# Two-layer decode block: the pass between layers in halves, another route for its q, and new order tables

## The chip, the core and the metric

The kernel runs on one core of one Trainium2 chip. The metric is the device time of one execution in microseconds, lower is better. A core has five engines with a queue each, worked off strictly in order: PE (TensorE, matrix products into the accumulation banks, PSUM), DVE (VectorE), ACT (ScalarE), POOL (GpSimd) and SP (SyncE, which here only issues DMA transfers from HBM to the on-chip memory, SBUF). Engines wait for each other through semaphores.

## The reference

Four sequences, one token each, pass through two layers; both layers use the same weights and the same caches.

```
for layer in (0, 1):
    q = layernorm(x) @ wq                       # 512 -> 32 heads x 128
    s = q . k_cache / sqrt(128)                 # 8 kv heads, 4 q heads on each, 4096 keys
    x = x + (softmax(s) . v_cache) @ wo         # 4096 -> 512
    n = layernorm(x)
    x = x + (sigmoid(n @ w_gate) * (n @ w_up)) @ w_down   # 512 -> 1792 -> 512
```

All arrays are bfloat16. K and V of one sequence and one kv head are 1 MiB each; there are 4 x 8 of each.

## The kernel before

**Tiles and slots.** K and V come in whole 1 MiB loads into 12 slots of SBUF, and later also into the four quarters of the tile that holds wq, once wq is needed no more (`yield_wq`). A table (`KEPT`) says which K and V of layer 0 stay in their slots until layer 1 uses them; the rest are loaded twice. wo (8 loads), w_gate, w_up and w_down stay resident. In all SP issues 115 loads, and two of the four short stores at the end.

**Order.** Nothing is ordered at run time. Three tables of letters fix everything. `ORDER` lists the 32 pairs of units as layer, sequence, pair (a unit is one kv head of one sequence). `LOADS` is the order of the transfers. `PROGRAM` is the order in which steps are issued, one letter each: `s` and `z` scores of the first and second unit of a pair, `t`, `u`, `T` parts of the transposition of a K on DVE, `m` `p` `n` `e` the maximum, its spreading, the bias and the exponentials, `P` `C` `D` the transposition of the probabilities and its copies, `h` `r` `i` the sums, `a` half a unit of probabilities times V, `o` (at the end `N`) the normalisation, `w` products with wo, `f` `F` `l` the turning of their result, `b` the block layout of q for a pair, and `.` the next step of a pass. After every letter `pump` issues each load of `LOADS` whose slot has been given up; SP then waits until the last reader of the slot has finished.

**The pass.** When a sequence has finished layer 0, a pass of 18 steps (`pass_steps`) brings it to layer 1: layer norm (`ln_a`, `ln_b`), gate product (`gate_row`), up product (`up_row`), `h_turn`, w_down (`down`, two parts), layer norm again, then q for layer 1. Products with one row as the stationary operand (128 x 1) are put on four strips of 32 columns of the array: each strip holds its own part of the outputs, in output rows 0, 32, 64 and 96 of a bank. `strips` is the constant with the four columns of the identity that pick these rows. There are four passes, spread over layer 0 and the first part of layer 1.

- `up_row` (L857-882): 16 matmuls a pass; then one DVE operation on 128 x 512 forms (tanh + 1) x up in `row_sb[:, 0]` (L877).
- `h_turn` (L884-903): four matmuls turn these rows to columns in one bank, one DVE copy (L899).
- `down` (L990-1018): 56 matmuls of one column; the first part makes output chunks 0 and 1, the second 2 and 3; one DVE operation adds the result to x.
- `first_q` (L929-933): q of the first pair of units needed in layer 1, 16 matmuls of 256 columns on four strips (L908) and a DVE copy. `first_turn` (L935-941): two matmuls (L922) and a DVE copy (L938) make columns of it. `first_spread` (L1022) with `spread_of` (L959): eight matmuls (L963) bring these to the layout that `b` reads.
- `other_half` (L943): the other kv half, 16 matmuls of 512 columns, ACT copy. `other_quarter` (L947): the remaining quarter, 16 matmuls of 256 columns on four strips (L908), DVE copy of 128 x 256 (L950). `others_turn` (L953): six matmuls and a copy. `others_spread` (L1034): 16 matmuls and an ACT copy. The last pass's `other_quarter` is the last reader of wq.

**The end.** The last pair's products with V finish layer 1. The last V comes in two halves. Then wo, the last layer norm and the last MLP for all four sequences follow (`last_unit`, `gate`, `up_half`); the change leaves these functions alone.

Of the kernel before, what the change touches and what calls it, by code (L numbers as in the profile page):

```python
# [133 lines left out]
sttzuumtpwnePtub szhubmpDrneTCihP saTazbaa swwmpDneotztCmtrihatPaapanorTCbDia  # L134
saettaawhozrwbixxwPCDmT swfzpaamFlnaeaow.w.pn.hr.P.e..ih.D.CP.aa.aw.a.b. sDrCzTobi.m.u
spzanaePbamphuaCr.on.DiaaaatehPTu soDCzmuxwtbpr sziwnmeaaaapxonbPher shzCwDfTPirwmaapbT
saaFlConzwm.iwtwue..wbDphuaaPraa.tt.w.C sz.n.Dmoe.piahwTabanPw.raCwoi st.zaDam.e.b.h
szptmaPaDoCrnib..w.aapeawaPThruDC.n sozewiabma sphunPaaztCbworewimDpTwaftwahaaFt
sPCroilzbDneahwmapaParoiCnDwaae.aawPhCD.T.Tor. s..zi.mauawpw.neu.bta.awPot.D sCw.hzw.mbw.r
sipzbanetama.apTPthr.CoD stwniezhmaa.P.abpan sCDzorimaTaapbattewP sDzhCnoebrhimtaaPapatDornwC  # L140
seiafaaaPTzohCrFlimapbnDeaaaohwrPCwT.wt swiwt...zD.m.apaanao.e.bhT.rPT sD.iz.C.aawm.pbn.
szmae..aP.h.orbpCw szwDbniehaTaaa smTPzCorTpiDnamaapenPbhraeo stizwDCmpbttnahPDtaaw
sazrCeoiPhaDmrapanaCewowfwwiPFCaaDaahlaoarXaiaNwY
"""


def bass_interleave_layers__gqa_block_cached__glu_gated_glu__decode_kernel(
# [228 lines left out]
    def dve(fn, reads=(), writes=()):  # L376
        return S.inst("dve", fn, reads=reads, writes=writes)
# [479 lines left out]
    def up_row(part):  # L857
        fns = []
        wv = wu_sb.rearrange("p k (f d) -> p k f d", d=2 * P)
        for k in range(2 * part, 2 * part + 2):  # L860
            for st in range(4):
                nt = (KW - st + 3) // 4
                fns.append(
                    (lambda k, st, nt: lambda e: e.matmul(
                        M_ps[1][32 * st:32 * st + 1, 0:nt * 2 * P],
                        lhsT=xc_bf[:, k, 0:1],
                        rhs=wv[:, k, bass.ds(st, nt, step=4), :],
                        start=(k == 0),
                        stop=(k == KD - 1),
                    ))(k, st, nt)  # L870
                )
# [4 lines left out]
        dve(  # L876
            lambda e: e.scalar_tensor_tensor(  # L877
                out=row_sb[:, 0, :], in0=t_row[:, :], scalar=1.0, in1=M_ps[1][:, :], op0=ALU.add, op1=ALU.mult
            ),
            reads=["rc", "rd", "rb", "M1"],  # L880
            writes=["ra"],
        )

    def h_turn():  # L884
        fns = []
        for t in range(2):
            for e_ in range(2):
                fns.append(
                    (lambda t, e_: lambda e: e.matmul(
                        M_ps[0][:, bass.ds(8 * t + e_, 4, step=2)],  # L890
                        lhsT=row_sb[:, 0, bass.ds(2 * P * t + e_, P, step=2)],
                        rhs=strips,
                        start=True,
                        stop=True,
                    ))(t, e_)
                )
        S.group("pe", fns, reads=["ra"] + IDENT, writes=["M0"])
        dve(
            lambda e: e.tensor_copy(hT_bf[:, :, 0], M_ps[0][:, 0:KF]),  # L899
            reads=["M0"],  # L900
            writes=["rc", "rd"],
        )

# [30 lines left out]

    def first_turn():  # L935
        S.group("pe", turned(2 * P, 0, 2), reads=["ra"] + IDENT, writes=["M0"])
        dve(
            lambda e: e.tensor_copy(qT_sb[:, 0:2 * REP], M_ps[0][:, 2 * P:2 * P + 2 * REP]),  # L938
            reads=["M0"],
            writes=["rb"],  # L940
        )
# [5 lines left out]
    def other_quarter(n0):  # L947
        S.group("pe", q_group(M_ps[1], n0 // 2, 2 - 2 * (n0 % 2), 2, range(KD)), reads=Q_READS, writes=["M1"])
        dve(
            lambda e: e.tensor_copy(row_sb[:, 1, 0:2 * P], M_ps[1][:, 0:2 * P]), reads=["M1"], writes=["rc", "rd"]  # L950
        )

    def others_turn():  # L953
        S.group("pe", turned(0, 0, 4) + turned(4 * REP, 1, 2), reads=["ra", "rc", "rd"] + IDENT, writes=["M0"])
# [4 lines left out]
    def spread_of(N, quadrants):  # L959
        S.group(  # L960
# [8 lines left out]
                ))(t, a, 64 * (t // 2) + t % 2)  # L969
                for t in range(NT4) for a in quadrants  # L970
            ],
# [17 lines left out]

    def down(b0, nb, part):  # L990
        xkeys = [f"x{b}" for b in range(b0, b0 + nb)]
        fns = []
        for c in range(2 * part, 2 * part + 2):
            for k in range(KF):
                fns.append(
                    (lambda c, k: lambda e: e.matmul(
                        M_ps[0][:, 128 + c * nb:128 + (c + 1) * nb],
                        lhsT=wd_sb[:, k, cols(c)],
                        rhs=hT_bf[:, k, 0:nb],
                        start=(k == 0),  # L1000
                        stop=(k == KF - 1),
                    ))(c, k)
                )
        rd = ["rc", "rd"] + wkeys["wd"]
        if part == 0:
            S.group("pe", fns, reads=rd, writes=["M0"])
            return
        S.last_write["M0"] = S.group("pe", fns, reads=rd)
        assert nb == 1
        dve(  # L1010
# [3 lines left out]
            ),  # L1014
            reads=["M0", "rs"] + xkeys,
            writes=xkeys,
        )

    def pass_steps(b0):
        n0 = seq[2 * firsts[1, b0]][2] // 2  # L1020

        def first_spread():  # L1022
            spread_of(2 * REP, range(2))
            begun.add(b0)
# [9 lines left out]
        def others_spread():  # L1034
            spread_of(6 * REP, range(4))
            act(
# [15 lines left out]
            h_turn,  # L1052
            lambda: down(b0, 1, 0),
            lambda: down(b0, 1, 1),
            lambda: ln_a(b0, 1),
            lambda: first_q(n0),
            first_turn,
            first_spread,
            second_sums,
# [699 lines left out]
```

## Time and profile before

| | us |
|---|---|
| median of three runs | 304.23 |
| the three runs | 305.87, 304.23, 302.63 |
| the profiled execution | 303.62 |
| its span, first to last instruction | 301.8 |
| PE busy | 218.2 |
| DVE busy | 192.8 |
| ACT busy | 122.0 |
| mean granted TensorE clock | 0.703 of full speed |

The profile is one execution, recorded by the hardware. "Busy" counts the time in which an engine works on an instruction. A row of a group gives source line, engine, operation, output and inputs, shape and count, then the time busy and the mean duration of one in ns, then the idle time just before and what ended it. PE's matmuls are pipelined, so durations of neighbours overlap. The 40 slices are 7.5 us each; a digit is the busy share in tenths, PEclk the granted clock in tenths. In rows of windows the DMA share may exceed 1, since packets overlap.

### The profile page before, as it was taken

To read this page: it belongs to the slowest core of one execution; us is meant where nothing else is said; L and a number is where in the kernel's file an instruction comes from. 1 tells how busy PE (TensorE), PEld (TensorE's weight loads), DVE (VectorE), ACT (ScalarE), POOL (GpSimd) and SP (SyncE) were. 2 spreads that over 40 slices of the span, in tenths; PEclk is the share of its full clock that TensorE was granted. 3 is DMA by queue.
4 is the path that set the end of the run, shared out by engine and by line. 5 is a ranking of instruction groups with operands and counts; after the bars stand their busy time and mean duration, and the time that the engine had idled before them with its cause. 6 is when DMAs were issued, how large, how long until landed. Compare 5 with 4: busy or idle time off the path is not lost. (4 is left out here: it accounts for less than half of the span.)

```text
span 301.8 us, 11397 instructions
## 1 busy us (share of the span) xinstructions
PE 218.2 (72%) x4904; PEld 150.9 (50%) x4904; DVE 192.8 (64%) x447; ACT 122.0 (40%) x421; POOL 42.6 (14%) x213
## 2 busy tenths in 40 slices
PE   1232373136779878797997979988988787888996
PEld 1221242122537555464655566744656564456685
DVE  6376757035543868668765767887585776497553
ACT  1010422410542374434444575325456352456830
POOL 0001111001000202111012110110311010122000
PEclk9999999999995757757565556675555595555555
DMA  7999999999999999999999999999999999999920
GB/s 287 422 427 419 414 395 397 398 384 422 413 404 418 417 421 419 418 410 395 414 372 421 397 418 423 417 417 417 385 421 420 419 393 376 416 418 418 414 95 3
DMA packets 20361, 117.38 MB, mean 389 GB/s; under 512 B 1876, under 2 KB 5976, under 8 KB 7640
## 3 DMA queue, kind: packets, MB, share of 16 engines
q1 hardware_dynamic: 20288, 116.66, 95.3%
q8 instruction: 38, 0.62, 0.8%
q14 instruction: 11, 0.09, 0.1%
q10 hardware_dynamic: 24, 0.01, 0.0%
HBM read 116.66 MB, written 0.00 MB: 387 GB/s over the span
## 5 line engine op out<-in xcount | busy, mean ns | idle before, releaser
L1081 DVE STREAM_TRANSPOSE slot<-slot 128x2048 f32<-128x2048 f32 (+2 forms) x69 | 102.8, 1495 | 29.0 <-DMA slot<-in_A_k_cache_dram 27.4
L1228 ACT ACTIVATE pT<-PT 32x128 bf16<-32x128 f32 x232 | 62.2, 268 | 60.4 <-PE PT L1173 26.5
L1273 PE MATMUL O_ps<-pT,slot 128*128 128x4 bf16 x1856 | 59.1, 166 | 21.3 <-DVE small L1253 12.8
L1273 PEld LDWEIGHTS O_ps<-pT,slot 128*128 128x128 bf16 x1856 | 55.2, 103 | 31.2 <-issue 17.9
L1097 PE MATMUL S_ps<-slot,qz 128*16 128x256 bf16 x992 | 61.4, 395 | 12.9 <-DVE slot L1081 5.8
L1155 ACT ACTIVATE wide<-S_ps,small 128x256 bf16<-128x256 f32 x64 | 33.2, 519 | 38.8 <-DVE small L1146 24.2
L1097 PEld LDWEIGHTS S_ps<-slot,qz 128*16 128x16 bf16 x992 | 27.7, 114 | 31.3 <-DVE slot L1081 9.6
L734 POOL COPY qz<-qs 32x32 bf16<-32x32 bf16 x112 | 22.9, 204 | 124.0 <-PE S_ps L1097 86.7
L1190 POOL TENSOR_TENSOR small<-small 128x8 bf16<-128x8 f32 (+1 forms) x96 | 19.3, 201 | 120.7 <-ACT wide L1155 84.0
L1114 DVE TENSOR_REDUCE small<-S_ps 128x2 bf16<-128x512 f32 x32 | 21.5, 671 | 7.7 <-PE S_ps L1097 5.4
L1173 PE MATMUL PT<-ident_bf,wide 128*128 128x64 bf16 (+1 forms) x288 | 18.4, 224 | 7.9 <-ACT pT L1228 3.8
L1173 PEld LDWEIGHTS PT<-ident_bf,wide 128*128 128x128 bf16 x288 | 14.7, 119 | 13.6 <-ACT wide L1155 5.0
L1139 DVE SCALAR_TENSOR_TENSOR O_ps<-O_ps,small,wide 128x128 f32<-128x128 f32 x32 | 10.9, 342 | 10.3 <-PE O_ps L1123 9.9
L908 PE MATMUL M_ps<-wq,small 128*1 128x256 bf16 (+1 forms) x192 | 15.4, 483 | 1.4 <-issue 1.4
L1330 PE MATMUL AC<-wo,oT 128*1 128x512 bf16 x96 | 11.9, 577 | 5.0 <-DMA wo<-in_A_wo_dram 2.6
L1155 ACT ACTIVATION_READ_ACCUMULATOR wide<-S_ps,small 128x1 f32 x64 | 12.3, 192 | 0.0
L1123 PE MATMUL O_ps<-ident_bf,small 128*128 128x64 bf16 x64 | 8.5, 223 | 5.2 <-DVE small L1114 5.2
L1146 DVE TENSOR_REDUCE small<-O_ps 128x2 f32<-128x128 f32 x32 | 9.3, 292 | 3.1 <-DVE O_ps L1139 0.5
L1123 PEld LDWEIGHTS O_ps<-ident_bf,small 128*128 128x128 bf16 x64 | 4.3, 107 | 11.9 <-DVE small L1114 8.8
L1304 DVE TENSOR_TENSOR oT<-O_ps,small 128x8 bf16<-128x8 f32 (+1 forms) x32 | 5.2, 162 | 6.6 <-PE O_ps L1273 6.4
L908 PEld LDWEIGHTS M_ps<-wq,small 128*1 128x1 bf16 x192 | 5.4, 114 | 7.5 <-issue 5.7
L839 PE MATMUL M_ps<-wg,small 128*1 128x512 bf16 (+1 forms) x64 | 8.2, 558 | 0.9 <-DVE small L503 0.9
(150 smaller groups left out, 198.2 us busy)
## 6 DMA issues: line engine op xcount, KB each, us to landing
slot<-in_A_v_cache_dram SPq DMA_DIRECT2D x50, 1024.0 KB, 9.2
slot<-in_A_k_cache_dram SPq DMA_DIRECT2D x43, 1024.0 KB, 10.3
wq<-in_A_wq_dram SPq DMA_DIRECT2D x2, 2048.0 KB, 9.8
wo<-in_A_wo_dram SPq DMA_DIRECT2D x8, 512.0 KB, 15.9
wq<-in_A_v_cache_dram SPq DMA_DIRECT2D x2, 1024.0 KB, 12.5
wq<-in_A_k_cache_dram SPq DMA_DIRECT2D x2, 1024.0 KB, 12.6
wg<-in_B_w_gate_dram SPq DMA_DIRECT2D x2, 896.0 KB, 12.9
wu<-in_B_w_up_dram SPq DMA_DIRECT2D x2, 896.0 KB, 11.3
```

The lines of the kernel that those rows point to most:

```text
L734: (lambda a, ps: lambda e: e.tensor_copy(qz_sb[ps, :, :, a, :], qs_sb[b][ps, :, c0:c0 + 2 * REP].rearrange("p t (u r) -> p u t r", r=REP), ...
L908: (lambda k, st: lambda e: e.matmul(M[32 * st:32 * st + 1, 0:nj * P], lhsT=xc_bf[:, k, 0:1], rhs=q_rows[:, k, h, j0:j0 + nj, st, :], start ...
L1081: dve(lambda e: e.transpose(kf, kf), writes=[f"s{st}"])
L1097: (lambda t, b2, e_, c, x1, r0: lambda e: e.matmul(S_ps[p][r0:r0 + 4 * REP, half], lhsT=qz_sb[:, part, t, :, :].rearrange("p a r -> p (a r)"),
L1114: dve(lambda e: e.tensor_reduce(rm_bf, S_ps[p].rearrange("p (u n) -> p u n", u=2), AX.X, ALU.max), reads=[f"S{p}"], writes=["rmb"])
L1123: (lambda u: lambda e: e.matmul(O_ps[n][:, P + 64 * u:P + 64 * u + 64], lhsT=rm_bf[:, u:u + 1].broadcast_to([P, P]), rhs=valid_bf, start=T ...
L1155: (lambda u, half: lambda e: e.activation(pe_sb[:, half], S_ps[p][:, half], ACTF.Exp, bias=nm_sb[:, u:u + 1], scale=scale, accum_out=sm_sb ...
L1173: (lambda w, a0, a1, c0: lambda e: e.matmul(PT[:, c0:c0 + 16 * (a1 - a0)], lhsT=wide_sb[:, NV + 64 * w:NV + 64 * w + P], rhs=valid_bf[:, : ...
L1190: (lambda out, a, b, op: lambda e: e.tensor_tensor(out, a, b, op))(out, a, b, op),
L1228: (lambda dst, frm: lambda e: e.activation(dst, frm, ACTF.Copy))(dst, frm),
L1273: (lambda n, x, c, j: lambda e: e.matmul(bank[:, ul * REP:(ul + 1) * REP], lhsT=vv[:, x * JG + c * 4 + j, :], rhs=pT[:, x % 2, ul, j, 2 * ...
L1330: (lambda r, h, i: lambda e: e.matmul(AC[32 * r:32 * r + 1, :], lhsT=oT_sb[:, h, own_column:own_column + 1], rhs=wo_sb[:, h, :], start=(j ...
```

## The change

1. **Up product in halves.** Two DVE operations of 128 x 256 take the place of one of 128 x 512; the second writes to the other half of `row_sb`.
2. **`h_turn` in halves.** Its four matmuls become two groups of two, one into each of the banks M0 and M1, and there are two copies, of 8 and of 6 columns, into `h_pass`.
3. **`down` in halves of the contraction.** Part 0 takes the first 8 of 14 chunks of h for all four output chunks, part 1 the other 6. It is still 56 matmuls.
4. **First pair's q.** `first_turn` and its copy go. `first_spread` takes the rows themselves as the stationary operand: 16 matmuls of four columns. A pass has 17 steps now.
5. **Last quarter of q.** 8 matmuls of 512 columns on two strips; the DVE copy takes 128 x 512; its turn takes four matmuls where it took two.
6. **New tables** `ORDER`, `LOADS` and `PROGRAM`. `KEPT` stays, and with it the set of loads. Among the pairs, 100 and 102 change places, 121 goes ahead of 111, and 133 ahead of 131. wo and the MLP weights come earlier in `LOADS`; at its end the last three K are loaded next to each other, before the last seven V.

```diff
 ORDER = """
-003 002 001 000 011 013 101 010 012 102 100 022 021 023 112 020 110 103 030 032 120 031 123 033 111
-121 113 131 133 130 132 122
+003 002 001 000 011 013 101 010 012 100 102 022 021 023 112 020 110 103 030 032 120 031 123 033 121
+111 113 133 131 130 132 122
 """
 LOADS = """
-kkkvkkvkkk oovkovvovk oogookkvvu guddvvkkvv kkvvkkvvvk vkvkvkvvkv vkvvkkvvvk kkvvkvvkkv vkkvkvkvvv
-kkvvkkvkvv kvkvkkvvvv vv
+ovkkokovko kkvvokkkkk oovvovkuvg guddvvkkvv kkvkvkvvkv vkvkvkvvvv kkvvkkvvvk kvkvkkvvvk vkkvkvvkvv
+kkvkvkvkvv kvkkkvvvvv vv
 """
 PROGRAM = """
...
-szmae..aP.h.orbpCw szwDbniehaTaaa smTPzCorTpiDnamaapenPbhraeo stizwDCmpbttnahPDtaaw
-sazrCeoiPhaDmrapanaCewowfwwiPFCaaDaahlaoarXaiaNwY
+s.CD.zmbi..aa.wTp..aan.ehT sPo.z.mb.rpi sCDne..auaha.z.rumPaCoiwpbDn sztmweaapThPaaoDnCbew
+swzrmihbaapaPraCTownwi sezTDmbaahpPnwDaarCoi saePDTzahmapnaCeowriwafFaPalhraCoDaiXaaNwawwY
 """
...
+    h_pass = t_bf[:, 2 * P:2 * P + KF]
...
-        dve(
-            lambda e: e.scalar_tensor_tensor(
-                out=row_sb[:, 0, :], in0=t_row[:, :], scalar=1.0, in1=M_ps[1][:, :], op0=ALU.add, op1=ALU.mult
-            ),
-            reads=["rc", "rd", "rb", "M1"],
-            writes=["ra"],
-        )
+        for n in range(2):
+            cs = slice(2 * P * n, 2 * P * n + 2 * P)
+            part_keys = (["ra"], ["rc", "rd", "rb"])[n]
+            dve(
+                (lambda n, cs: lambda e: e.scalar_tensor_tensor(
+                    out=row_sb[:, n, 0:2 * P], in0=t_row[:, cs], scalar=1.0, in1=M_ps[1][:, cs],
+                    op0=ALU.add, op1=ALU.mult,
+                ))(n, cs),
+                reads=["M1"],
+                writes=part_keys,
+            )
 
     def h_turn():
...
+        for t in range(2):
+            ks = slice(8 * t, min(8 * t + 8, KF))
+            dve(
+                (lambda t, ks: lambda e: e.tensor_copy(h_pass[:, ks], M_ps[t][:, ks]))(t, ks),
+                reads=[f"M{t}"],
+                writes=[f"h{t}"],
+            )
...
-    def first_turn():
-        S.group("pe", turned(2 * P, 0, 2), reads=["ra"] + IDENT, writes=["M0"])
-        dve(
-            lambda e: e.tensor_copy(qT_sb[:, 0:2 * REP], M_ps[0][:, 2 * P:2 * P + 2 * REP]),
-            reads=["M0"],
-            writes=["rb"],
+    def first_spread():
+        S.group(
+            "pe",
+            [
+                (lambda t, j, a: lambda e: e.matmul(
+                    M_ps[1][32 * a:32 * a + 32, 8 * t + 4 * j:8 * t + 4 * j + 4],
+                    lhsT=row_sb[:, 0, bass.ds(P * j + 64 * (t // 2) + t % 2, 32, step=2)],
+                    rhs=strips,
+                    start=True,
+                    stop=True,
+                ))(t, j, a)
+                for t in range(NT4) for j in range(2) for a in range(2)
+            ],
+            reads=["ra"] + IDENT,
+            writes=["M1"],
         )
...
     def other_quarter(n0):
-        S.group("pe", q_group(M_ps[1], n0 // 2, 2 - 2 * (n0 % 2), 2, range(KD)), reads=Q_READS, writes=["M1"])
-        dve(
-            lambda e: e.tensor_copy(row_sb[:, 1, 0:2 * P], M_ps[1][:, 0:2 * P]), reads=["M1"], writes=["rc", "rd"]
-        )
+        h, j0 = n0 // 2, 2 - 2 * (n0 % 2)
+        S.group(
+            "pe",
+            [
+                (lambda k, st: lambda e: e.matmul(
+                    M_ps[1][32 * st:32 * st + 1, :],
+                    lhsT=xc_bf[:, k, 0:1],
+                    rhs=q_rows[:, k, h, j0:j0 + 2, 2 * st:2 * st + 2, :],
+                    start=(k == 0),
+                    stop=(k == KD - 1),
+                ))(k, st)
+                for k in range(KD) for st in range(2)
+            ],
+            reads=Q_READS,
+            writes=["M1"],
+        )
+        dve(lambda e: e.tensor_copy(row_sb[:, 1, :], M_ps[1][:, :]), reads=["M1"], writes=["rc", "rd", "rb"])
...
-    def down(b0, nb, part):
+    def down(b0, part):
+        fns = [
+            (lambda c, k: lambda e: e.matmul(
+                M_ps[0][:, 128 + c:129 + c],
+                lhsT=wd_sb[:, k, cols(c)],
+                rhs=h_pass[:, k:k + 1],
+                start=(c == 0 and k == 0),
+                stop=(c == KD - 1 and k == KF - 1),
+            ))(c, k)
+            for c in range(KD) for k in range(8 * part, min(8 * part + 8, KF))
+        ]
```

More of the change, by code (lines that the diff above doesn't have):

```diff
@@ L969, in spread_of @@
                 ))(t, a, 64 * (t // 2) + t % 2)
[L970 removed]
+                for t in range(NT4) for a in range(4)
             ],
@@ L988, in scales @@
         )
-    def down(b0, nb, part):
[L991 to L1004, printed above, removed]
+    def down(b0, part):
[8 more added lines that the diff above has]
+            for c in range(KD) for k in range(8 * part, min(8 * part + 8, KF))
+        ]
         if part == 0:
-            S.group("pe", fns, reads=rd, writes=["M0"])
+            S.group("pe", fns, reads=["h0"] + wkeys["wd"], writes=["M0"])
             return
-        S.last_write["M0"] = S.group("pe", fns, reads=rd)
-        assert nb == 1
+        S.last_write["M0"] = S.group("pe", fns, reads=["h1"] + wkeys["wd"])
         dve(
```

64 lines of the change are left out of this document (34 added, 30 removed).

## The prediction

> **What bounds the kernel now.** I began with the page: busy shares, the 40 slices, the queues.
>
> ```profile
> span 301.8 us, 11397 instructions
> PE 218.2 (72%) x4904; PEld 150.9 (50%) x4904; DVE 192.8 (64%) x447; ACT 122.0 (40%) x421; POOL 42.6 (14%) x213
> ...
> PE   1232373136779878797997979988988787888996
> ...
> PEclk9999999999995757757565556675555595555555
> DMA  7999999999999999999999999999999999999920
> GB/s 287 422 427 419 414 395 397 398 384 422 413 404 418 417 421 419 418 410 395 414 372 421 397 418 423 417 417 417 385 421 420 419 393 376 416 418 418 414 95 3
> ...
> q1 hardware_dynamic: 20288, 116.66, 95.3%
> ```
>
> The DMA row stands at 9 from the second slice to the 38th, so the kernel is a stream of 116.66 MB with a tail behind it. Undisturbed slices move some 422 GB/s: a 1 MiB load, which is one K or V, takes 1.049 MB / 422 = 2.48 us of stream. PE is close behind from slice 13 on, at a granted clock of 0.5 to 0.7. Next, the windows: the steady stretch first whole, then cut where slices of the GB/s row dip.
>
> ```profile
> 93.00:260.00 167.00, 141.39 (x3121) 96.63 (x3121) 118.64 (x276) 79.60 (x276) 27.42 (x135) 0.59 1.01 409
> ...
> 140.00:172.00 32.00, 28.35 (x643) 19.46 (x644) 22.21 (x54) 16.13 (x57) 6.29 (x31) 0.60 1.00 399
> 203.00:217.00 14.00, 11.79 (x262) 7.55 (x254) 8.37 (x16) 7.58 (x26) 2.62 (x13) 0.50 1.00 402
> 239.00:259.00 20.00, 16.48 (x351) 10.88 (x347) 14.77 (x41) 6.91 (x23) 2.02 (x10) 0.67 0.99 389
> ```
>
> The columns are length, busy time of PE, weight loads, DVE, ACT and POOL, then clock, DMA share and GB/s. Against 422 GB/s, 167 us at 409 lose 5.1 us. Three stretches hold most of it: 32 x (1 - 399/422) = 1.7 us, 14 x (1 - 402/422) = 0.7 us, 20 x (1 - 389/422) = 1.6 us. Over the whole stretch PE idles 167 - 141.4 = 25.6 us, and DVE 48.4 us. Last, what makes a dip: the SP queue's timeline, one landing, and the chain of waits.
>
> ```profile
> 239.47 3.19 SPq L373 DMA_DIRECT2D slot<-in_A_k_cache_dram  x2
> ...
> slot<-in_A_k_cache_dram SPq DMA_DIRECT2D x1, 1024.0 KB, 6.3
> ...
> 242.33 6.80 DMA slot<-in_A_k_cache_dram
> 249.13 0.02 issue
> 249.15 2.31 DVE slot L1081
> ```
>
> The first K, issued at 239.47, took 6.3 us and landed at 245.8. The next was issued at 242.33, only 3.4 us before that, and landed at 249.13: 3.4 us behind its predecessor instead of 2.48. So a slot that comes free late costs up to a microsecond, though a load is still in flight. The chain then stays on compute to the end: stream and PE are both near their limit.
>
> **A rule weighed.** The Trainium skill, "DMA: Bandwidth & Descriptors" (the two cost components), puts the fixed cost of a transfer at some 2.0 us, so that an issue 3.4 us ahead should leave no gap. The measured gap differs, and the measurement decides. By the page the tables could gain or lose nothing through issue times; that is part of the third rival.
>
> **The change, part by part.** The sum starts at the profiled execution's 303.62 us (its span is 301.8), 0.6 below the median of 304.23 and inside the runs' 302.63 to 305.87.
>
> *The last quarter of q.* Each of four passes turns 16 matmuls of 256 columns on four strips into 8 of 512 on two; its copy grows from 256 to 512 columns.
>
> ```profile
> 252.34 1.06 PE L908 MATMUL M_ps<-wq,small 128*1 128x256 bf16 x16
> ...
> 258.15 2.73 PE L908 MATMUL M_ps<-wq,small 128*1 128x512 bf16 x32
> ...
> L908 PE MATMUL M_ps<-wq,small 128*1 128x256 bf16 x128 | 8.5, 412 | 1.4 <-issue 1.4
> L877 DVE SCALAR_TENSOR_TENSOR t_row<-t_row,M_ps 128x512 bf16<-128x512 f32 x4 | 2.7, 673 | 1.8 <-PE M_ps L864 1.7 <-ACT t_row L852 0.2
> L950 DVE CAST t_row<-M_ps 128x256 bf16<-128x256 f32 x4 | 1.7, 425 | 5.5 <-PE M_ps L908 5.5
> ```
>
> Sixteen matmuls of 412 ns finish in 1.06 us, so four strips run side by side. The group of 32 is 16 of 512 columns and the old quarter's 16: 2.73 - 1.06 = 1.67 us for four rounds of 512 columns. No row has two strips; if two run side by side as four do, the new quarter is again four rounds of 512: 1.67 us, for which 0.85 was spent (half the columns). That is +0.85 us of PE per pass at this clock. The bounds are half of it, at the full clock, and 1.7 us more, if strips do not pair up; I take +0.85, since the 0.5 clock rules where three of four passes stand. DVE gains 0.673 - 0.425 = 0.25, taking L877 as the nearest 512-wide row. Here the Trainium skill speaks the other way: "TensorEngine Tiling (Array Packing)", Instruction Overhead, gives each matmul some 60 cycles of overhead, and by it half as many matmuls would be the cheaper group. The rows show no such overhead between strips, only columns.
>
> In all 4 x 1.1 = 4.4 us on two engines. What hides it is the 25.6 us of PE idle above. That cover is gone in the last pass: there the chain runs through these very matmuls.
>
> ```profile
> 251.52 1.03 PE S_ps L1097 x13
> 252.55 0.89 PE M_ps L908 x15
> 253.43 0.02 issue
> 253.45 0.44 DVE t_row L932
> 253.89 0.05 issue
> 253.94 0.22 PE M_ps L922 x2
> ...
> 258.22 2.66 PE M_ps L908 x32
> ```
>
> I take one pass of four: **+1.1** (0 to +4.4). Queued behind the longer group on PE are score and P·V products, and on SP the four loads that wait for the last quarter to give up wq.
>
> *The first pair's q.* The turn (0.22, L922) and its copy (167 ns below) go, with about 0.1 of hand-over: 0.5 saved. Sixteen spread matmuls stand for eight.
>
> ```profile
> L963 PE MATMUL M_ps<-t_row,ident_bf 128*32 128x8 bf16 x32 | 1.1, 171 | 0.3 <-DVE t_row L938 0.3
> L938 DVE CAST t_row<-M_ps 128x8 bf16<-128x8 f32 x4 | 0.7, 167 | 1.9 <-PE M_ps L922 1.9
> L899 DVE CAST t_row<-M_ps 128x14 bf16<-128x14 f32 x4 | 0.8, 191 | 1.5 <-PE M_ps L889 1.5
> ```
>
> Four passes' eights are busy 1.1 us together, 0.27 each; eight more add at most that, and I take 0.1, since most of 0.27 is one pipe's drain. The gain reaches the path only where nothing else fills PE; in the last pass: **-0.4** (0 to -1.6).
>
> *Halves.* Before, product 0.67, turn some 0.25 (a group as short as L922's 0.22), copy 0.19: w_down can start 1.11 us after the up product. After, two products of 256 columns, each between L950's 0.43 and half of L877's 0.67, and two copies of about 0.17 stand on DVE in the order product, product, copy, copy: the first copy ends at 0.43 + 0.43 + 0.17 = 1.03. The second (1.28) hides under the first half of w_down. Gain 0.08 per pass, against 0.34 more DVE time: **0** (-0.3 to +1.4, if DVE were the bound).
>
> *The tables.* The same 117 issues of SP, the same bytes, the same K and V kept. I counted in both orders of instructions, for each load that reuses a slot, how many loads lie between it and the newest one that its slot's release must wait for. A small number means a late issue. For the 65 loads from the 40th on the mean is 3.88 in both. Two stand in before: loads 61 and 67, inside 140 to 172; after, 61, 67 and also 99, inside the 239 to 259 stretch. Loads 85 and 86 (203 to 217) go from three and three to four and three. By the stretches: +0.9 for a third two (1.7 / 2), -0.7 for the 203 to 217 dip: **+0.2** (-4.0, all three dips closed, to +2.6, three more twos).
>
> *The tail.*
>
> ```profile
> 268.13 0.70 SPq L373 DMA_DIRECT2D slot<-in_A_v_cache_dram  x1
> ...
> slot<-in_A_v_cache_dram SPq DMA_DIRECT2D x1, 512.0 KB, 22.1
> ...
> 290.65 1.07 PE L1273 MATMUL S_ps<-slot,slot 128*128 128x4 bf16 x32
> 291.58 0.57 PE L1423 MATMUL O_ps<-oT,wo 128*128 128x4 bf16 x16
> ```
>
> The last half V lands at 268.13 + 22.1 = 290.2. PE takes it up at 290.65, with both halves' products (0.93) and then w_o of the unit before (0.49) still to do. In the new order half the products and this w_o stand ahead of the last half. Were PE free at the landing, 0.4 + 0.47 + 0.49 = 1.3 us would go. It is late now, but wq's slots are given up two loads earlier and three K loads then go ahead of the last seven V's, so I take **-0.9** (0 to -1.3).
>
> Sum: 303.62 + 1.1 - 0.4 + 0 + 0.2 - 0.9 = 303.6 us.
>
> **Rivals.** *PE sets the pace.* From 93 us on its longer quarter is not absorbed in any pass: +4.4, with +0.9 for load 99 and no gain in the tail: 303.62 + 5.3 = 308.9. For it: PE busy 85% there, and the chain's compute end. Against it: the DMA share of 1.01 in the same row. It decides once the idle that a pass finds is under 1.1 us.
>
> *The tables close the dips.* -4.0, tail -1.3, first pair -0.4: 297.9. For it: the dips are late issues, and several first pair's chains get shorter. Against it: the same mean distance, and one two more.
>
> *Nothing reaches the end.* Dips that are not due to issue times, a tail still limited by PE, every edit under PE idle: 303.6 within 0.5. It lies within the forecast's own range.
>
> **How the numbers follow.** Forecast with the third rival 0.50, own range 301.2 to 306.5; dips closed 0.27; PE's pace 0.23. About 1% is what a measurement tells from no change here. Nearly all of the first case is within that; the second is faster and the third slower. The range, 299.0 to 308.0, leaves a tenth on each side.
>
> **What would show it.** Quarter: eight matmuls in about 1.7 us at the 0.5 clock; under 1.0 refutes me. First pair: its spread directly behind L932's copy. Halves: the first copy behind the second product on DVE. Tables: a gap of about 0.9 us before the 99th load's landing; GB/s in the three stretches near 399, 402, 389. Tail: w_o of the last pair's first unit ahead of the last half V. I am wrong if those stretches rise above 415, or if PE's idle from 93 to 260 falls by 4 us and the stream's GB/s with it.

## The result and the profile after

The changed kernel takes 306.73 us (median of 20 runs, 303.81 to 310.53); the kernel before, on the same chip, takes 303.98 (20 runs, 302.63 to 307.26). The ratio is 1.0067 with a 95% interval of [1.0043, 1.0092]; it leaves out executions over 1.5% slower than the fastest of their kernel, which is why it lies under the quotient of the medians. The forecast was 303.6 us, a hair from no change. The time is inside its range and inside the 1% that it called no change, but the interval excludes 1: the change costs some 2.0 us.

The profiled execution took 303.81 us, the fastest of the twenty, so its page shows the changed kernel at its best. First the page: span, engines, clock, GB/s by slice, and the queue that carries instructions.

```profile
span 302.0 us, 11426 instructions
PE 221.4 (73%) x4904; PEld 150.3 (50%) x4904; DVE 194.5 (64%) x448; ACT 121.6 (40%) x421; POOL 42.4 (14%) x213
...
PEclk9999999999995766557567556855665575757555
...
GB/s 296 405 409 404 411 403 420 391 410 417 413 400 424 418 406 378 422 420 409 418 410 422 397 419 419 414 420 421 365 384 418 426 375 388 411 417 421 416 129 5
...
q8 instruction: 39, 0.64, 0.8%
```

TensorE is busy 3.2 us longer, DVE 1.7. The dips of the GB/s row are still there, in other slices: 378 in the sixteenth, 365 and 384 around 220 us, 375 and 388 around 250 us. Then the windows, of this profile and of a second one of the same kernel (after_again below), whose span of 305.1 us is nearer to the median.

```profile
93.00:260.00 167.00, 145.65 (x3138) 96.59 (x3135) 120.65 (x279) 79.56 (x277) 27.23 (x135) 0.61 1.00 408
140.00:172.00 32.00, 28.11 (x653) 18.98 (x653) 22.30 (x53) 15.33 (x55) 6.24 (x31) 0.64 1.01 413
203.00:217.00 14.00, 10.96 (x223) 6.60 (x219) 8.50 (x14) 5.97 (x21) 1.82 (x9) 0.50 0.99 397
239.00:259.00 20.00, 18.97 (x327) 11.35 (x325) 15.39 (x42) 7.53 (x25) 2.02 (x10) 0.60 1.00 392
```

```profile
93.00:260.00 167.00, 145.98 (x3096) 95.70 (x3094) 119.97 (x278) 78.93 (x277) 26.64 (x133) 0.58 1.00 403
```

TensorE's idle from 93 to 260 us fell from 25.6 to 21.4 us and 21.0 us, by some 4.4 us; about half of that is the four longer quarters (below). In the fastest execution the stream hardly moved with it (409 to 408 GB/s). In the other it fell to 403: against 409 that is 167 x (1 - 403/409) = 2.4 us, of the 3.2 us by which that execution (306.88) lies over its batch's median of the kernel before (303.65). This is the sign of being wrong that the prediction had set.

The edited operations and, below, the chain of waits in the last pass:

```profile
L970 PE MATMUL M_ps<-wq,small 128*1 128x512 bf16 x32 | 6.4, 543 | 0.0
...
L880 DVE SCALAR_TENSOR_TENSOR t_row<-t_row,M_ps 128x256 bf16<-128x256 f32 x8 | 2.9, 404 | 2.1 <-PE M_ps L864 2.1
L982 DVE CAST t_row<-M_ps 128x512 bf16<-128x512 f32 x4 | 2.8, 689 | 4.1 <-PE M_ps L970 4.0
```

```profile
255.35 1.71 PE M_ps L917 x16
257.06 1.58 PE M_ps L970 x8
...
258.67 7.15 DMA wq<-in_A_v_cache_dram
```

Eight matmuls on two strips take 1.58 us and stand on the chain as forecast. Over the four passes L970 is busy 6.4 us, 1.6 a pass, where sixteen matmuls of 256 columns were busy 8.5 / 8 = 1.06 before: 0.54 us more a pass, less than the 0.85 forecast. So the quarter's own time on TensorE does not explain the loss by being larger than was thought. What the prediction missed is where time comes to count.

### The profile page after: what moved, and what is told of

It is laid out like the page before. It is cut to its first block, busy times and chain, and to the rows that moved or that the text cites. A ratio compares the mean times of both kernels' runs of the same rounds, so it can differ in the third digit from the quotient of the medians.

```text
span 302.0 us, 11426 instructions
## 1 busy us (share of the span) xinstructions
PE 221.4 (73%) x4904; PEld 150.3 (50%) x4904; DVE 194.5 (64%) x448; ACT 121.6 (40%) x421; POOL 42.4 (14%) x213
## 5 line engine op out<-in xcount | busy, mean ns | idle before, releaser
L1115 DVE STREAM_TRANSPOSE slot<-slot 128x1024 f32<-128x1024 f32 (+2 forms) x67 | 100.0, 1501 | 21.6 <-DMA slot<-in_A_k_cache_dram 19.0
L1262 ACT ACTIVATE pT<-PT 32x128 bf16<-32x128 f32 x236 | 63.3, 268 | 58.7 <-PE PT L1207 30.7
L1131 PE MATMUL S_ps<-slot,qz 128*16 128x256 bf16 x976 | 60.2, 391 | 21.2 <-DVE slot L1115 11.8
L1307 PEld LDWEIGHTS O_ps<-pT,slot 128*128 128x128 bf16 x1856 | 56.0, 103 | 23.4 <-issue 9.1
L1307 PE MATMUL O_ps<-pT,slot 128*128 128x4 bf16 x1856 | 59.8, 166 | 10.2 <-DMA slot<-in_A_v_cache_dram 2.5
L1131 PEld LDWEIGHTS S_ps<-slot,qz 128*16 128x16 bf16 x976 | 26.6, 110 | 41.2 <-DVE slot L1115 16.4
L917 PE MATMUL M_ps<-wq,small 128*1 128x256 bf16 (+1 forms) x128 | 11.5, 506 | 0.0
L852 ACT ACTIVATE t_row<-M_ps,small 128x512 f32<-128x512 f32 x4 | 2.8, 688 | 17.3 <-DVE small L538 12.7
L1287 DVE RECIPROCAL small<-O_ps 128x8 f32<-128x8 f32 x31 | 6.1, 198 | 5.1 <-PE O_ps L1276 4.8
```

What stands on the lines that cost most here:

```text
L917: (lambda k, st: lambda e: e.matmul(M[32 * st:32 * st + 1, 0:nj * P], lhsT=xc_bf[:, k, 0:1], rhs=q_rows[:, k, h, j0:j0 + nj, st, :], start ...
L1115: dve(lambda e: e.transpose(kf, kf), writes=[f"s{st}"])
L1131: (lambda t, b2, e_, c, x1, r0: lambda e: e.matmul(S_ps[p][r0:r0 + 4 * REP, half], lhsT=qz_sb[:, part, t, :, :].rearrange("p a r -> p (a r)"),
L1262: (lambda dst, frm: lambda e: e.activation(dst, frm, ACTF.Copy))(dst, frm),
L1307: (lambda n, x, c, j: lambda e: e.matmul(bank[:, ul * REP:(ul + 1) * REP], lhsT=vv[:, x * JG + c * 4 + j, :], rhs=pT[:, x % 2, ul, j, 2 * ...
```

## The experiments

All ratios are to the kernel before, run on the same chip in the same batch (303.2 to 303.7 us), with 95% intervals. Loads are numbered in SP's order from 0. A load's lead is the time from its issue to the landing of the load before it.

### Which part costs the time

**code_only**: the changed kernel with the old `ORDER`, `LOADS` and `PROGRAM`, and a step without work where `first_turn` was, so that the old `PROGRAM` fits.

```diff
             lambda: first_q(n0),
+            lambda: None,
             begin,
```

> The new code under the old tables (a step without work stands where the first turn was). Against the kernel before the change cost +0.7%, some 2 us. Theory Q, the two-strip quarter is what costs: it is in here, so +2 us, ratio 1.005 to 1.01. Theory T, the new tables cost: they are not in here, ratio 0.997 to 1.002.

Measured: 1.0036 [1.0005, 1.0067].

**tables_only**: the kernel before with the new tables; turn and spread are one step.

```diff
-            first_turn,
-            first_spread,
+            begin,
...
+        def begin():
+            first_turn()
+            first_spread()
```

> The old code under the new tables (first turn and first spread in one step). Q: ratio 0.995 to 1.002, since the quarter is still on four strips. T: +2 us, ratio 1.005 to 1.01.

Measured: 1.005 [1.0017, 1.0082].

**four_strips**: the changed kernel with the last quarter of q as it was.

```diff
     def other_quarter(n0):
...
+        S.group("pe", q_group(M_ps[1], n0 // 2, 2 - 2 * (n0 % 2), 2, range(KD)), reads=Q_READS, writes=["M1"])
```

> The changed kernel with the last quarter of q back on four strips (16 matmuls, copy of 256 columns, two turning matmuls). Q: the loss goes, ratio to before 0.995 to 1.002; the quarter takes 0.85 us on PE where two strips took 1.6 to 1.7. T: ratio 1.005 to 1.01, as the whole change.

Measured: 1.002 [0.9993, 1.0047].

**two_strips**: the kernel before with `other_quarter` and `others_turn` of the changed one, and nothing else.

```diff
     def other_quarter(n0):
-        S.group("pe", q_group(M_ps[1], n0 // 2, 2 - 2 * (n0 % 2), 2, range(KD)), reads=Q_READS, writes=["M1"])
+        h, j0 = n0 // 2, 2 - 2 * (n0 % 2)
...
+                for k in range(KD) for st in range(2)
```

> The kernel before with nothing but the quarter on two strips. Q: 0.8 us per pass on PE, ratio 1.003 to 1.01. T: ratio 0.998 to 1.003, the longer group hidden by idle time of PE.

Measured: 1.0124 [1.009, 1.0157], about 3.8 us, and the largest of all. Two things follow. The quarter is the costly part: without it the changed kernel is at 1.002. And the effects don't add: the quarter alone costs more than the whole change, and all code edits together (code_only) cost a third of what it costs alone.

**code_four** (code_only with the old quarter: the halves and the first spread), **spread_only** and **halves_only** (one of the two), and **wide_copy** (the quarter's DVE copy 512 columns wide, of which half is read by nobody):

```diff
-            lambda e: e.tensor_copy(row_sb[:, 1, 0:2 * P], M_ps[1][:, 0:2 * P]), reads=["M1"], writes=["rc", "rd"]
+            lambda e: e.tensor_copy(row_sb[:, 1, :], M_ps[1][:, :]), reads=["M1"], writes=["rc", "rd", "rb"]
```

> The new code under the old tables, but with the last quarter of q on four strips as before: what is left is the halves and the first spread. The quarter alone cost 1.24%, all of the new code under the same tables 0.36%. If parts add up, these two parts gain 0.9%: ratio 0.988 to 0.995, about 301 us. If they do not add up (each change of a few tenths of a us merely moves where loads are issued late), ratio 0.997 to 1.005.

> The kernel before with nothing but the first pair's q spread straight from its rows. If parts add up: 0.5 us of chain saved in passes where nothing fills PE, ratio 0.994 to 0.999. If not: 0.997 to 1.005.

> The kernel before with nothing but the halves (up product, h_turn, w_down). By the order on DVE only 0.08 us per pass is gained and 0.3 us of DVE time added: ratio 0.998 to 1.003. If the halves carry the gain of the parts: 0.991 to 0.997.

> The kernel before, four strips as before, but the copy of the quarter takes 128 x 512 where 128 x 256 holds what is used (the other half is what the bank held, and nothing reads it). If PE's 0.85 us is what the quarter costs: ratio 0.998 to 1.003. If DVE's 0.25 us is: 1.005 to 1.012.

Measured: 1.0023 [1.0004, 1.0042], 1.0012 [0.999, 1.0034], 1.001 [0.998, 1.0039] and 1.0003 [0.9977, 1.0028]. DVE's share of the quarter, the halves and the spread each cost nothing that could be told from none. The halves and the spread together (code_four) cost 0.7 us, with an interval of 0.1 to 1.3, and did not gain.

### Which passes pay

**two_last** and **two_first**: two strips in the last pass alone, and in the first three alone. **quarter_twice**: the old 16 matmuls issued twice in a row, for more TensorE time on four strips. **two_strips_again**: two_strips once more.

```diff
-            other_quarter(n0)
+            (two_quarter if b0 == 3 else other_quarter)(n0)
```

```diff
-        S.group("pe", q_group(M_ps[1], n0 // 2, 2 - 2 * (n0 % 2), 2, range(KD)), reads=Q_READS, writes=["M1"])
+        S.group("pe", q_group(M_ps[1], n0 // 2, 2 - 2 * (n0 % 2), 2, range(KD)) * 2, reads=Q_READS, writes=["M1"])
```

> The kernel before with the quarter on two strips in the last pass alone. As predicted, that only this pass pays (+1.1 us): ratio 1.002 to 1.005 here and 1.000 in the three others. If every pass pays the same: a quarter of 1.24%, 1.003. If the last pass carries the whole loss: 1.009 to 1.016.

> The kernel before with the quarter on two strips in the first three passes. Only the last pass pays: ratio 0.998 to 1.002. Every pass pays: 1.007 to 1.012.

> The kernel before with the 16 matmuls of the last quarter issued twice, the second time over the first: the same result, 32 matmuls of 256 columns on four strips, 1.7 us of PE where 0.85 were, as on two strips, with the old copy. If PE's time is what two strips cost: ratio 1.008 to 1.016. If it is something else of the two strips: 0.998 to 1.004.

> The same as two_strips, a second time, since that one had four runs: ratio 1.009 to 1.016 if it holds; under 1.006 if the first was a chance.

Measured: two_last 1.0019 [0.9998, 1.0039], two_first 1.0105 [1.0077, 1.0134], quarter_twice 1.0098 [1.0067, 1.0129], two_strips_again 1.0143 [1.011, 1.0175]. So the three passes with idle time around them cost 3.2 us, where the forecast had them free. The pass in which the chain runs through these matmuls costs 0.6 us, with an interval of -0.1 to 1.2 that holds the forecast's 1.1 as well as nothing; in the profiled execution its eight matmuls met a granted clock of 1.00 and took 1.03 us. quarter_twice came out where it was expected if TensorE's time is the cost. But it also puts 32 instructions a pass into TensorE's list (16 matmuls, each with a weight load), so it changes two things.

The traces show one place. TensorE's timeline in the kernel before, at 179 us:

```profile
179.21 0.19 PE L1242 MATMUL O_ps<-small 128*128 128x8 bf16 x2
179.62 1.01 PE L1423 MATMUL O_ps<-oT,wo 128*128 128x1 bf16 x32 [0.22 <-DVE oT L1304]
180.75 1.20 PE L1273 MATMUL O_ps<-pT,slot 128*128 128x4 bf16 x32
```

The same 32 products in two_strips:

```profile
178.60 0.19 PE L1264 MATMUL O_ps<-small 128*128 128x8 bf16 x2
178.95 0.42 PE L1445 MATMUL O_ps<-oT,wo 128*128 128x1 bf16 x10 [0.16 <-DVE oT L1326]
182.13 0.73 PE L1445 MATMUL O_ps<-oT,wo 128*128 128x1 bf16 x22 [2.76 <-issue]
182.72 0.99 PE L1295 MATMUL O_ps<-pT,slot 128*128 128x4 bf16 x32
```

After the tenth of 32 like products, which need nothing new, TensorE stands still for 2.76 us, and "issue" says that it waited for nothing that the profile shows. The gap stands at the same instruction (number 4987 of TensorE's matmuls and weight loads in order of time) in two_strips_again (2.51 us) and two_first (2.73 us), and in no other trace so far. What it does to the stream is seen in SP's timeline, first before, then two_strips:

```profile
182.02 1.61 SPq L373 DMA_DIRECT2D slot<-in_A_v_cache_dram  x2
187.09 0.33 SPq L373 DMA_DIRECT2D slot<-in_A_k_cache_dram  x1
```

```profile
183.79 1.61 SPq L373 DMA_DIRECT2D slot<-in_A_v_cache_dram  x2
188.86 0.33 SPq L373 DMA_DIRECT2D slot<-in_A_k_cache_dram  x1
```

Loads 74 to 76 go out 1.77 us later, and load 76 follows its predecessor after 3.41 us instead of 2.49. By load 80 the stream is 1.6 us behind that of the kernel before, having been 0.4 us ahead at load 74: 2.0 us lost. It ends 3.1 us behind; most of the rest is lost at load 94, which was issued in time (a lead of 8.06 us). This trace has two more gaps of the kind, 1.41 us before 214.7 us and 1.65 before 236.8.

Why does TensorE stop? The two-strip quarter has eight matmuls fewer, and its turn two more; each brings a weight load, so TensorE's list of instructions is 12 shorter in each pass (page of two_strips: x4880 and x4880, against x4904 and x4904). The q8 row of each page counts packets of instructions: 38 in the kernel before, 0.62 MB, so 16 KB each, one for 9808 / 38 = 258 of TensorE's records. One of these packets moved near 176 us in the kernel before. In two_strips none moved from 171.5 to 179.5 us; it came at 179.8, and TensorE went on 2.3 us later. The theory: a block of instructions came late, and TensorE ran out of them. The rival: the quarter's own TensorE time.

### Place in the list against time

The next runs set the two against each other: more work with the old places, and less work with shifted places.

**two_padded**: two_strips, and ahead of the quarter in each pass six matmuls of four columns, whose results the real ones overwrite; with their weight loads they put the 12 instructions back.

```diff
+            [
+                (lambda k, st: lambda e: e.matmul(
+                    M_ps[1][32 * st:32 * st + 1, 0:4],
+                    lhsT=xc_bf[:, k, 0:1],
+                    rhs=q_rows[:, k, h, j0, 2 * st, 0:4],
+                    start=True,
+                    stop=True,
+                ))(k, st)
+                for k in range(KD - 1) for st in range(2)
+            ]
+            + [
```

> The kernel before with the quarter on two strips in every pass (1.0124 and 1.0143 by itself), and ahead of its 8 matmuls six of four columns, whose results the real ones overwrite. The two-strip quarter and its turn make TensorE's list 12 instructions shorter a pass (6 matmuls with 6 weight loads); the six put them back, so that all behind stands again at the numbers that it has in the kernel before. The work only grows. If the loss is the stall of 2.5 to 2.8 us in the middle of the products with w_o at TensorE's instruction 4987 (about 179.5 us), because a block of its instructions came late: no stall there, an instruction packet near 176 us again, ratio at most 1.004. If the loss is the quarter's 0.85 us a pass of TensorE: 1.012 to 1.016, and loads 74 to 78 issue late all the same.

**short_quarter**: the kernel before with 10 of the quarter's 16 matmuls.

```diff
-        S.group("pe", q_group(M_ps[1], n0 // 2, 2 - 2 * (n0 % 2), 2, range(KD)), reads=Q_READS, writes=["M1"])
+        S.group("pe", [f for i, f in enumerate(q_group(M_ps[1], n0 // 2, 2 - 2 * (n0 % 2), 2, range(KD))) if not 4 <= i < 10], reads=Q_READS, writes=["M1"])
```

> The kernel before with 10 of the quarter's 16 matmuls (two of the four parts of the contraction are left out, one of them for two strips only, so that part of q is wrong in value): TensorE has less work by 0.3 us a pass, and its list is shorter by the same 12 instructions a pass as on two strips. If the place of the instructions in the list makes the stall: a gap of over 2 us at TensorE's instruction 4987, ratio 1.008 to 1.013 in spite of the smaller work. If TensorE's time makes the loss: no gap, ratio 0.997 to 1.001.

**short_padded**: short_quarter with the six small matmuls ahead (the lines are cut at the dots).

```diff
-        S.group("pe", [f for i, f in ...
+        S.group("pe", small + [f for i, f in ...
```

> The quarter with 10 of its 16 matmuls again (1.0094; part of q is wrong in value), now with the six small matmuls ahead, so that TensorE's list is as long as in the kernel before and its work within 0.1 us a pass of the short one. If the 1.0094 came from the place of the instructions alone: no gap at instruction 4987, ratio 0.997 to 1.002. If leaving the six out costs in another way (order of the engines, what is read when): 1.006 or more.

Measured: short_quarter, with less work than the kernel before, 1.0094 [1.0061, 1.0128]; short_padded, the same with the places restored, 1.001 [0.9985, 1.0035]; two_padded 1.0074 [1.0045, 1.0103], against 1.0124 and 1.0143 without the small ones. The same products in short_quarter's timeline, then in short_padded's, then in two_padded's:

```profile
179.04 0.43 PE L1423 MATMUL O_ps<-oT,wo 128*128 128x1 bf16 x10 [0.16 <-DVE oT L1304]
182.22 0.73 PE L1423 MATMUL O_ps<-oT,wo 128*128 128x1 bf16 x22 [2.75 <-issue]
```

```profile
179.49 1.01 PE L1434 MATMUL O_ps<-oT,wo 128*128 128x1 bf16 x32 [0.22 <-DVE oT L1315]
```

```profile
179.71 1.01 PE L1455 MATMUL O_ps<-oT,wo 128*128 128x1 bf16 x32 [0.22 <-DVE oT L1336]
```

(The trace of short_quarter is of an execution of 309.62 us; its median is 307.10.) The gap comes and goes with the number of instructions ahead of it, whichever the work. The queues say the same. In short_quarter from 171 to 179.5 us no instruction packet moved, and the view has no q8 row; from 179.5 to 181 us one did:

```profile
q1 hardware_dynamic: 489, 3.59, 101.3%
```

```profile
q1 hardware_dynamic: 86, 0.61, 98.0%
q8 instruction: 1, 0.02, 4.1%
```

In the kernel before, it moved between 174 and 178 us:

```profile
q1 hardware_dynamic: 225, 1.62, 99.6%
q8 instruction: 1, 0.02, 1.4%
```

That a list shorter by these instructions makes this stall is shown, and that it alone costs 0.8 to 0.9% (short_quarter against short_padded and against the kernel before). But two_padded kept 0.7% where at most 0.4% was expected. Its trace loses 1.7 us of its final 2.0 at loads 83 to 88, behind the third pass's quarter. The timeline there, of the kernel before and of two_padded:

```profile
204.82 0.38 PE L908 MATMUL M_ps<-wq,small 128*1 128x256 bf16 x4
206.62 0.81 PE L908 MATMUL M_ps<-wq,small 128*1 128x256 bf16 x12 [1.41 <-issue]
```

```profile
205.43 0.19 PE L952 MATMUL M_ps<-wq,small 128*1 128x4 bf16 x4
206.78 0.17 PE L952 MATMUL M_ps<-wq,small 128*1 128x4 bf16 x2 [1.16 <-issue]
```

The kernel before has a stall of its own, in the quarter of the third pass; the longer quarter comes on top of it. The lead of load 85 was 4.15 us in the kernel before (issued at 211.24) and 2.42 in two_padded (issued at 212.54). **two_longer**, two_strips with twelve small matmuls instead of six, was to move that stall away too:

```diff
-                for k in range(KD - 1) for st in range(2)
+                for k in range(KD - 1) for st in (0, 1, 0, 1)
```

> The quarter on two strips with twelve small matmuls ahead instead of six (1.0074): the list is 12 instructions a pass longer than in the kernel before, as it is with the spread straight from the rows (1.0012), whose trace has neither the stall at 4987 nor the one of 1.2 to 1.4 us near 205 us that before and two_padded have. If the quarter's longer time costs only where it comes on top of such a stall (load 85 was 2.42 us ahead in two_padded, 4.15 in the kernel before): no gap over 1 us near 205 us, load 85 over 3.3 us ahead, ratio at most 1.004 in spite of still more work. If the time costs by itself: 1.007 to 1.010.

Measured: 1.0066 [1.0038, 1.0093], and this is a miss: the stall stayed.

```profile
205.54 0.38 PE L1205 MATMUL PT<-ident_bf,wide 128*128 128x32 bf16 x4
207.59 0.42 PE L1205 MATMUL PT<-ident_bf,wide 128*128 128x64 bf16 x5 [1.68 <-issue]
```

Load 85 went out at 213.88 with a lead of 1.73 us and landed 4.76 us behind its predecessor. spread_only, whose list is as much longer, has no such stall. So the place in the list is not all that decides when a block comes, and whether the longer quarter costs anything where no stall precedes it was not told by this run.

The trace of quarter_twice tells more. From 80 us to the end TensorE has no gap without a named cause over 0.7 us in it. The third pass's quarter and the issue of load 85:

```profile
206.01 1.88 PE L908 MATMUL M_ps<-wq,small 128*1 128x256 bf16 x32
```

```profile
211.66 0.33 SPq L373 DMA_DIRECT2D slot<-in_A_v_cache_dram  x1
```

Load 85 had a lead of 3.08 us and landed 3.67 us behind its predecessor; the stream went from 0.7 us ahead of the kernel before at load 83 to 0.3 behind. So with a longer quarter this hand-over loses about 1 us without a stall too. The rest of what quarter_twice costs was not followed.

### The changed kernel itself

**after_again** is the changed kernel once more, **after_padded** the same with the six small matmuls of two_padded ahead of the quarter; its instructions then stand at the numbers that they have in four_strips.

> The changed kernel once more on this chip, for a profile of an execution that is nearer its median, and as the measure for the padded one. Both theories: 1.0043 to 1.0092. If instructions come late in its slower executions: a gap of over 1 us on TensorE that no wait explains, at a place where its first profile has none. If not: no such gap, and loads that land late behind late issues, spread over the passes.

> The changed kernel with the same six small matmuls ahead of the quarter in each pass. Its instructions then stand at the numbers that they had with the quarter on four strips (1.002 [0.9993, 1.0047]), and TensorE's work only grows. If the changed kernel's loss (1.0067) against that one is a matter of where its instructions stand: at most 1.004. If it is TensorE's time on the quarter: 1.006 to 1.009.

Measured: after_again 1.0104 [1.007, 1.0138], after_padded 1.0026 [0.9988, 1.0064]. With more work the loss is gone but for what four_strips has too: the medians of this batch are 307.12 us and 304.96. Against the first measurement (1.0067 [1.0043, 1.0092]) alone the padded kernel is not clearly faster. One place can be seen in the changed kernel's first profile, in TensorE's timeline and in SP's:

```profile
212.54 0.29 PE L1307 MATMUL O_ps<-pT,slot 128*128 128x4 bf16 x5
214.07 0.46 PE L1307 MATMUL O_ps<-pT,slot 128*128 128x4 bf16 x11 [1.23 <-issue]
```

```profile
210.56 0.33 SPq L373 DMA_DIRECT2D slot<-in_A_v_cache_dram  x1
214.60 0.33 SPq L373 DMA_DIRECT2D slot<-in_A_k_cache_dram  x1
```

TensorE stops after five of 16 products with V. Load 86, which takes the slot that these products give up, goes out at 214.60, 0.07 us behind the last of them, with a lead of 2.59 us. It lands 6.40 us later, at 221.00, 3.81 us behind load 85: 1.33 us more than the 2.48 of an undisturbed load, and the largest loss of one load in this trace. after_again has the same stall (1.23 us), load 86 at a lead of 2.91, and 4.34 us from load 85 to it. after_padded does not have it:

```profile
214.43 0.59 PE L1317 MATMUL O_ps<-pT,slot 128*128 128x4 bf16 x16
```

There load 86 had a lead of 3.82 us and landed 2.48 us behind load 85. But after_padded has two gaps without a named cause that the changed kernel has not, 1.05 us before 147.0 us and 1.06 before 265.9: such stalls move with the padding, they do not all go. Nor has all of the loss such a place. after_again had lost 1.9 us against the kernel before by load 56, most of it at load 49 (3.68 us behind its predecessor, though its lead was 4.92), some 10 us after a stall of 2.04 us at 106 us. But the first profile, four_strips and after_padded have this stall too (1.9 to 2.0 us) and lose less there (0.3 to 1.4 us by load 52).

## Why the prediction was wrong

**The terms that were off.** Without the quarter the prediction's sum is 303.62 - 0.4 + 0 + 0.2 - 0.9 = 302.5 us, 1.1 under the kernel before. four_strips is the change without the quarter: 1.002 [0.9993, 1.0047], which is 0.6 us over it, from -0.2 to 1.4. So the gains taken for the first pair's q and the tail did not come, and that makes some 1.7 us. The quarter takes the change from there to 1.0067, and in the second measurement to 1.0104: 1.4 or 2.5 us, each give or take some 1.2, where 1.1 was taken. In size, then, the gains that did not come are at least as much of the miss; the mechanism that failed is the quarter's.

**The quarter: the step that failed.** The prediction said that "what hides it is the 25.6 us of PE idle above" and that "that cover is gone in the last pass", and took one pass of four, +1.1. The duration was right: 1.58 us for the last pass's eight matmuls on two strips where 1.67 was taken, and a wide copy of 0.689 us where 0.673 was taken. (The increase was not: 0.85 is half of 1.67, while the prediction's own row has 1.06 us for the old sixteen, so by its rows it should have been 0.6.) Where it is paid was wrong. The first three passes, taken as covered, cost 3.2 us (1.0105); the last alone costs 0.6 (1.0019), which leaves its 1.1 open. And in the first passes the quarter's time need not be what costs: an edit with less work and the same change of the list's length (short_quarter) cost 2.9 us, and the same edit with the length restored (short_padded) none that can be measured. The prediction counted matmuls only to price their time, and never asked what becomes of the instructions behind them when their places in the list shift. In the changed kernel the list as a whole is no shorter (x4904 on both pages): the first spread puts in the twelve a pass that the quarter takes out, and the new tables order it anew. That place matters there as well is what after_padded shows.

**The idle time as cover.** TensorE's idle did fall by 4.2 us with the stream unmoved in the fastest execution, so such cover exists. But it is not a store from which any pass may draw. Behind the third pass's quarter the slack is a load's lead, 4.15 us at load 85 in the kernel before; a stall and a longer quarter together cut it to 2.42 in two_padded and 1.73 us in two_longer. In the first the stream lost 1.7 us there against the kernel before; in the second load 85 alone came 4.76 us behind its predecessor, where 2.68 stood before. quarter_twice, whose quarter takes 1.88 us there where sixteen matmuls take 1.06, has no large stall at either place, lost about 1 us at load 85 and took 1.0098, so that TensorE's time is not free; two_padded (1.0074), whose stall there is no longer than that of the kernel before, says the same. In the changed kernel it costs nothing that can be measured: after_padded, whose quarter is as long, has four_strips within its interval. What makes the difference was not found. All twenty traces together show what a lead is worth. Of the loads 40 to 109, 42 of 85 with a lead under 3.8 us landed more than 2.9 us behind their predecessor; of those with 3.8 to 6 us, 87 of 488; with more, 31 of 827. The 3.4 us in the prediction's example are no exception, and what was drawn there from the rule weighed, that such a lead leaves no gap, does not hold here.

**The first pair's q: -0.4.** Alone it gave 1.0012 [0.999, 1.0034], whose lower end is a gain of 0.3 us: that excludes the full -1.6 and, by a hair, the -0.4. No gain was seen.

**Halves: 0.** Right, as far as 1.001 [0.998, 1.0039] tells: the two products of 404 ns cost what was taken, between 0.34 and 0.43.

**The tables: +0.2.** Mis-sized: alone they cost 1.005, 1.5 us, inside the bounds of -4.0 to +2.6. Counting loads between a slot's use and its release did not give it. The 0.9 us forecast for load 99 did not appear, and of the three stretches one rose to 413 GB/s (from 399) while dips opened elsewhere. Beside the other edits they cost nothing that can be told: four_strips 1.002 and code_four 1.0023 differ in them alone. What causes the 1.5 us was not found.

**The tail: -0.9.** From the landing of the last half V to the end of the span the profile before takes 301.8 - 290.2 = 11.6 us, the first profile after 302.0 - 291.0 = 11.0 and after_again 305.1 - 293.3 = 11.8. The order is as forecast; a gain of 0.6 in one and a loss of 0.2 in the other do not establish the 0.9.

**The rivals.** The PE-bound rival had the sign, at 308.9, by letting each of four passes pay the quarter's time; after_padded speaks against that for the changed kernel, and quarter_twice and two_padded for it in the kernel before. No rival named a late block of instructions. What of the changed kernel's loss is shown: padding takes it from 1.0104 to 1.0026 in one batch, and the 1.23 us stall, with the 1.33 us lost at load 86, is absent in the padded trace. That all of the loss is of this kind is not shown.

## What to carry to other kernels

An edit that takes instructions out shifts all that follow in the engine's list, and in this long unrolled kernel that alone was worth 0.9%, as much as the whole change. Before a loss of this size is put down to the edit's work, pad it back to the old length with instructions that do next to nothing, or take as many out elsewhere, and look in the timeline for groups of like instructions that stop in the middle with "issue" behind the gap. And idle time counts as cover only where the next loads have lead to spare: read the lead at each hand-over, not the sum of the idle time. Gains in a sum need a run of their own as much as costs do: the change without its costliest part tells whether they came.

## What the runs showed of the hardware

TensorE's instructions come by DMA beside the data, in packets of 16 KB, one for about 258 matmuls and weight loads, some 6.5 us apart in the busy part. At eight gaps without a named cause (two_strips and short_quarter near 182 us, the kernel before, two_padded and two_longer near 207, the changed kernel near 214 and twice in after_again), TensorE went on 2.3 to 2.6 us after a packet began to move, though the packet itself took 0.9 to 1.1 us. In all twenty traces this holds for each of the 28 such gaps over 0.9 us from 60 us on. Most packets come with no such gap. That TensorE waited for these packets is inferred from this regularity. The Trainium skill, "Runtime: NRT & Kernel Launch" (Instruction fetch mechanics), says that instructions are refilled in blocks of 16 KiB, 256 instructions each, and calls the cost of a block's border mostly hidden. The block's size agrees with the trace. The cost does not always: TensorE stopped for 2.5 to 2.8 us at instruction 4987 in four traces of three kernels. What makes a block late was not found; the data queue takes 95% of the DMA engines' time in all of these kernels, and no run eased it.

Matmuls that write one row on two strips run in pairs, as those on four strips run in fours: in the chain of the changed kernel eight of 512 columns on two strips took 1.58 us and sixteen on four strips, four rounds as well, 1.71, at granted clocks of 0.58 and 0.50.
